# Giving PSUM banks to steps as the order is made, and moving pairs 12 to 15 of an attention stage off TensorE

## The chip, the cores and the metric

The kernel runs on one core of a Trainium2 chip. The metric is the time of one execution on the device in microseconds (us). Executions of one kernel differ by 1 to 2% here, so each comparison below rests on several runs of both kernels on the same chip. (A run is called slow when it took over 1.5% longer than the fastest of the same kernel in its rounds.) Matmul results are written to PSUM; SBUF holds the kernel's other tiles. TensorE is called PE, VectorE DVE, ScalarE ACT, GpSimd POOL, as in the profile.

## The reference

```python
# q, k, v: (8, 8, 576, 64) float32: 8 batches, 8 heads, 576 tokens, 64 wide
# 1. q, k, v are averaged over groups of 4 tokens: an attention over 144 tokens,
#    its output repeated 4 times
# 2. a local attention: token i sees tokens i-3 .. i+3 (masked softmax)
# 3. x = (1 + 2), laid out as 4608 tokens x 512
# 4. h = x @ w_in (512 x 2048);  g = h - tanh(h);  y = g @ w_out (2048 x 512)
```

Two heads of a batch are handled together, as a "pair": 32 pairs, four to a batch. Steps 1 to 3 are the *attention*, step 4 is the *dense* part: nine blocks of 512 tokens, 1152 matmuls of 512 columns.

## The kernel before

The author writes every step as an operation with an estimated time, the buffers that it reads and writes, and a priority. A small list scheduler in the kernel's own Python makes one fixed order from them. A recording layer below (the tile framework) takes the instructions in that order and works out from the tiles that they touch which engine must wait for which semaphore.

The kernel uses PSUM as eight banks of 512 float32 columns each. Before, they have roles, and each role is a tile of its own:

```python
    ps_ts = fixed("ps_ts", [128, 2, 512], FP32, pool=psum)      # two banks: transposes, scores
    ps_ox = fixed("ps_ox", [128, 2, 512], FP32, pool=psum)      # two banks: outputs, transposes back
    # at the start two more pairs, ps_ts1 and ps_ox1; later, in their place:
        ps_hy.extend(fixed("ps_hy", [128, 512], FP32, 4, pool=pool))   # four banks for dense groups
```

One pair of heads goes through these steps (cut):

```python
    qr  <- cast and reorder of q, k              # POOL
    if p >= T_DMA:  qT <- DMA transpose of qr;  qk <- ACT copy
    else:           nine PE transposes into ps_ts;  qk <- ACT copy
    half, qkd <- q and k pooled over four tokens # POOL (DVE too for the first four pairs)
    scores -> ps_ts (from pair NEW on: all scores at once, over ps_ts and ps_ox)
    E <- exp                                     # ACT, reads two banks in one instruction
    E <- E * mask                                # DVE, pair 4 on: both inputs in SBUF
    outs -> ps_ox                                # PE
    r <- 1 / sums; ln <- outs * r                # DVE, each reads two banks in one instruction
    if p >= X_DMA:  lT <- DMA transpose of ln;  xT <- join of lT   # DVE or POOL
    else:           PE transposes into ps_ox; od <- ACT; xT <- DVE
    # the pooled v: PE matmuls with `pick` before pair NEW, adds on POOL from there on
    M2_FIRST, T_DMA, X_DMA, NEW, LATE = 12, 16, 16, 16, 0
```

The pooled q and k are written as two planes:

```python
    qkd = fixed("qkd", [128, 344], BF16, 2)
    eng.tensor_tensor(out=qkd[s][:, 0:2 * G].rearrange("p (i g) -> p g i", i=2),
                      in0=half[:, :, 0, :], in1=half[:, :, 1, :], op=ALU.add)
```

A dense group is four matmuls into one bank of `ps_hy`, a tanh on ACT that reads it, and a subtraction on DVE that reads it again; the second product gathers 16 matmuls in a bank and ACT copies it out.

The softmax here doesn't subtract the row's maximum and nothing guards it: scores larger than these inputs give would overflow.

## Time and profile before

| | before |
|---|---|
| time, median of 3 runs | 347.96 us (346.37 to 349.49) |
| span of the profiled run | 345.8 us |
| first dense matmul | 30.0 us |
| PE idle after it, in gaps of 0.2 us or more | 8.2 us in 6 gaps |

The page of the profile starts with busy times. Part 2 cuts the span into 40 slices; the PE row is the busy share in tenths, the PEclk row the granted TensorE clock in tenths. The last line is part 4, the chain of waits followed back from the end.

```profile
span 345.8 us, 6564 instructions
PE 323.4 (94%) x2479; PEld 164.9 (48%) x2520; DVE 218.5 (63%) x336; ACT 202.7 (59%) x334; POOL 182.9 (53%) x196
...
PE   8777999999969999899989998999999999999995
...
PEclk9998999999998999999999999999999999999999
...
PE 80%; DVE 7%; DMA 4%; ACT 4%; issue 2%; POOL 1%; DVEq 0%; ACTq 0%; POOLq 0%
```

PE is the limit and nearly full. What it loses, it loses at the start and in a few gaps.

The groups of instructions (line, engine, operation, tiles, shape, count; then busy us and mean ns of one, then idle time before them and its releasers) show two things: the mask multiply (L554, L568) and the pooled add (L495).

```profile
L495 POOL TENSOR_TENSOR qkd<-half 128x288 bf16<-128x288 f32 x30 | 46.0, 1535 | 3.2 <-DVE half L490 2.3
L554 DVE TENSOR_TENSOR E<-E,mask 128x960 bf16<-128x960 bf16 x28 | 34.1, 1216 | 14.6 <-ACT E L550 14.4
L568 DVE TENSOR_TENSOR E<-E,mask 128x192 bf16<-128x192 bf16 x28 | 17.3, 619 | 6.0 <-ACT E L561 5.7
L495 DVE TENSOR_TENSOR qkd<-half 128x288 bf16<-128x288 f32 x2 | 4.0, 2022 | 0.1
```

The timeline around one of the gaps (start us, duration us, engine, line, operation; in brackets the idle time before it and what ended it):

```profile
140.41 0.72 POOL L381 CAST vw<-vst 128x640 bf16<-128x640 f32 x1
...
140.47 3.58 DVE L554 TENSOR_TENSOR E<-E,mask 128x960 bf16<-128x960 bf16 x1 [0.17 <-ACT E L550]
...
141.09 1.49 POOL L495 TENSOR_TENSOR qkd<-half 128x288 bf16<-128x288 f32 x1
...
142.16 1.37 POOL L448 CAST qr<-qkn 128x1152 bf16<-128x1152 f32 x1
...
144.10 0.37 PE L579 MATMUL ps_ox<-vw,E 128*128 128x65 bf16 x5 [1.54 <-DVE E L554]
```

The multiply took 3.58 us; the shortest of its line took 0.65 us. It ended half a microsecond after an unbroken run of GpSimd instructions ended, and PE stood still for it.

### The profile page before, as it was taken

To read this page: it belongs to the slowest core of one execution; us is meant where nothing else is said; L and a number is where in the kernel's file an instruction comes from. 1 tells how busy PE (TensorE), PEld (TensorE's weight loads), DVE (VectorE), ACT (ScalarE), POOL (GpSimd) and SP (SyncE) were. 2 spreads that over 40 slices of the span, in tenths; PEclk is the share of its full clock that TensorE was granted. 3 is DMA by queue.
4 is the path that set the end of the run, shared out by engine and by line. 5 is a ranking of instruction groups with operands and counts; after the bars stand their busy time and mean duration, and the time that the engine had idled before them with its cause. 6 is when DMAs were issued, how large, how long until landed. Compare 5 with 4: busy or idle time off the path is not lost.

```text
span 345.8 us, 6564 instructions
## 1 busy us (share of the span) xinstructions
PE 323.4 (94%) x2479; PEld 164.9 (48%) x2520; DVE 218.5 (63%) x336; ACT 202.7 (59%) x334; POOL 182.9 (53%) x196
## 2 busy tenths in 40 slices
PE   8777999999969999899989998999999999999995
PEld 3453455555535555344444444454444444444442
DVE  4775885468876775859887987776765443344300
ACT  2864875668855866576666676677654444344411
POOL 7675748577677792859786978885600100000000
PEclk9998999999998999999999999999999999999999
DMA  7999999898537892999999999662321200110021
GB/s 238 287 262 207 240 255 242 224 303 223 155 104 198 219 240 79 233 203 243 237 247 230 237 239 228 138 139 61 81 59 48 72 32 30 51 40 32 30 83 68
DMA packets 99212, 56.51 MB, mean 163 GB/s; under 512 B 77678, under 2 KB 86382, under 8 KB 99182
## 3 DMA queue, kind: packets, MB, share of 16 engines
q1 hardware_dynamic: 94670, 51.32, 60.3%
q0 software_dynamic: 4224, 4.19, 7.4%
q10 hardware_dynamic: 288, 0.59, 0.6%
q8 instruction: 19, 0.31, 0.4%
q14 instruction: 11, 0.09, 0.1%
HBM read 42.46 MB, written 9.44 MB: 150 GB/s over the span
## 4 chain that ended last, share of the span: by engine, by line
PE 80%; DVE 7%; DMA 4%; ACT 4%; issue 2%; POOL 1%; DVEq 0%; ACTq 0%; POOLq 0%
PE ps_hy L661 34%; PE ps_hy L688 31%; DVE E L554 3%; PE ps_ox L579 3%; DMA w_out_sb<-in_moe_w_out_dram 3%; PE ps_ts L509 3%; PE ps_ts L476 2%; PE ps_ox L586 2%; PE ps_ts L837 2%; DMA out_dram<-y 2%; DVE qkd L495 1%; ACT qk L480 1%; PE ps_ox L614 1%; DVE E L568 1%; PE ps_ox L420 1%
## 5 line engine op out<-in xcount | busy, mean ns | idle before, releaser
L661 PE MATMUL ps_hy<-xT,w_in_sb 128*128 128x512 bf16 x562 | 144.5, 384 | 2.7 <-DVE xT L641 1.5
L688 PE MATMUL ps_hy<-w_out_sb,gT 128*128 128x512 bf16 x550 | 138.4, 379 | 1.9 <-DMA w_out_sb<-in_moe_w_out_dram 0.5
L672 DVE TENSOR_TENSOR gT<-ps_hy,u 128x512 bf16<-128x512 f32 x144 | 97.0, 686 | 66.5 <-ACT u L669 65.5
L669 ACT ACTIVATE u<-ps_hy 128x512 f32<-128x512 f32 x144 | 85.0, 599 | 89.8 <-PE ps_hy L661 89.5
L688 PEld LDWEIGHTS <-gT 128*128 128x128 bf16 x576 | 54.0, 98 | 62.8 <-issue 0.8
L661 PEld LDWEIGHTS <-w_in_sb 128*128 128x128 bf16 x576 | 54.1, 98 | 62.6 <-issue 3.8
L495 POOL TENSOR_TENSOR qkd<-half 128x288 bf16<-128x288 f32 x30 | 46.0, 1535 | 3.2 <-DVE half L490 2.3
L490 POOL TENSOR_TENSOR half<-qk 128x576 f32<-128x576 bf16 x29 | 34.7, 1198 | 18.9 <-ACT qk L480 13.9
L554 DVE TENSOR_TENSOR E<-E,mask 128x960 bf16<-128x960 bf16 x28 | 34.1, 1216 | 14.6 <-ACT E L550 14.4
L448 POOL CAST qr<-qkn 128x1152 bf16<-128x1152 f32 x28 | 33.7, 1204 | 14.7 <-PE ps_ts L476 9.2
L600 DVE TENSOR_TENSOR ln<-ps_ox,r 128x896 bf16<-128x896 f32 x30 | 32.6, 1088 | 0.8
L699 ACT COPY y<-ps_hy 128x512 f32<-128x512 f32 x36 | 21.1, 586 | 18.4 <-PE ps_hy L688 18.4
L550 ACT ACTIVATE E<-ps_ts 128x960 bf16<-128x960 f32 x30 | 29.1, 970 | 4.6 <-PE ps_ts L509 4.6
L381 POOL CAST vw<-vst 128x640 bf16<-128x640 f32 x32 | 26.4, 826 | 2.6 <-PE ps_ox L579 2.0
L480 ACT COPY qk<-ps_ts 128x1152 bf16<-128x1152 bf16 x14 | 15.7, 1118 | 14.6 <-PE ps_ts L476 14.6
L406 POOL TENSOR_TENSOR vp<-v 72x256 bf16<-72x256 f32 x16 | 12.4, 773 | 21.1 <-PE ps_ox L586 21.1
L579 PE MATMUL ps_ox<-vw,E 128*128 128x65 bf16 x300 | 18.9, 196 | 4.2 <-DVE E L554 4.2
L579 PEld LDWEIGHTS <-E 128*128 128x128 bf16 x320 | 16.4, 99 | 11.2 <-DVE E L554 5.7
L568 DVE TENSOR_TENSOR E<-E,mask 128x192 bf16<-128x192 bf16 x28 | 17.3, 619 | 6.0 <-ACT E L561 5.7
L402 POOL TENSOR_TENSOR v<-v 72x512 f32<-72x512 f32 x16 | 20.3, 1268 | 1.0
L467 ACT COPY qk<-qT 128x1152 bf16<-128x1152 bf16 x16 | 19.3, 1207 | 0.0
L624 POOL TENSOR_TENSOR xT<-lT 128x480 bf16<-128x480 bf16 x7 | 7.1, 1009 | 23.1 <-DMA lT<-ln 23.1
(89 smaller groups left out, 254.4 us busy)
## 6 DMA issues: line engine op xcount, KB each, us to landing
vst<-in_v_dram SPq DMA_DIRECT2D x62, 160.0 KB, 4.4
qkn<-in_q_dram SPq DMA_DIRECT2D x32, 288.0 KB, 4.7
out_dram<-y SPq DMA_DIRECT2D x36, 256.0 KB, 2.0
qkn<-in_k_dram SPq DMA_DIRECT2D x30, 288.0 KB, 4.8
v<-in_v_dram SPq DMA_DIRECT2D x16, 288.0 KB
w_in_sb<-in_moe_w_in_dram POOLq DMA_DIRECT2D x4, 512.0 KB, 10.5
w_out_sb<-in_moe_w_out_dram POOLq DMA_DIRECT2D x4, 512.0 KB, 9.6
qkn<-in_k_dram ACTq DMA_DIRECT2D x2, 288.0 KB
```

Source lines behind the costliest of these rows:

```text
L381: P.choice([(eng, ns, lambda fn=fn: fn(out=vw[w][:, 2 * jj:2 * jj + 2, :, 0:64], in_=vst[s])) for eng, ns, fn in CAST_V[p >= NEARLY]], rea ...
L448: op("POOL", 1300, lambda: GP.tensor_copy(out=qr[s].rearrange("p a (h d) -> p h a d", h=2), in_=qkn[sn].rearrange("p h (a d) -> p h a d", ...
L490: eng.tensor_tensor(out=half, in0=four[:, :, 0:2, :], in1=four[:, :, 2:4, :], op=ALU.add)
L495: eng.tensor_tensor(out=qkd[s][:, 0:2 * G].rearrange("p (i g) -> p g i", i=2), in0=half[:, :, 0, :], in1=half[:, :, 1, :], op=ALU.add)
L550: op("ACT", 960, lambda: A.activation(out=e1, in_=ps[:, :, 0:480], func=AF.Exp, scale=SCALE), reads=ts, writes=[("E", e, 0)], pri=pri)
L554: op("DVE", 950, lambda: V.tensor_tensor(out=e1, in0=e1, in1=mask[:, 0:480].unsqueeze(1).to_broadcast([128, 2, 480]), op=ALU.mult), reads= ...
L579: T.matmul(po[:, hh, 65 * t:65 * t + 65], E[e][:, c:c + 128], vw[w][:, 2 * jj + hh, t, :], start=True, stop=True)
L600: op("DVE", 1060, lambda: V.tensor_tensor(out=ln[s].rearrange("p n (h d) -> p h n d", d=D), in0=blocks[:, :, :, 0:64], in1=r[s].unsqueeze( ...
L661: T.matmul(ps_hy[slot], w_in_sb[:, dc, fc * 128:(fc + 1) * 128], xT[dc][:, kb * 512:kb * 512 + 512], start=(dc == 0), stop=(dc == N_DC - 1))
L669: op("ACT", 590, lambda: A.activation(out=u[us], in_=ps_hy[slot], func=AF.Tanh), reads=[("hy", slot)], writes=[("u", us)], pri=DPRI)
L672: op("DVE", 670, lambda: V.tensor_tensor(out=gT[g][:, fc, :], in0=ps_hy[slot], in1=u[us], op=ALU.subtract), reads=[("hy", slot), ("u", us) ...
L688: T.matmul(ps_hy[slot], gT[g][:, fc, ts * 128:ts * 128 + 128], w_out_sb[:, fc, :], start=(fc == 0), stop=(fc == N_FF - 1))
```

## The change

The intent: no fixed roles for banks. While the order is made, each step that fills PSUM is given the bank or the two banks that became free first, up to four banks for attention after the start ("b") and five for dense groups ("d"). With that the first pairs can overlap more, and priorities are set towards the end of batch 0, so that dense work starts sooner. Pairs 12 to 15 are also moved to the form that pairs 16 and later have. The diff, cut to its core:

```diff
+class Banks:
+    def __init__(self, n, kind, key): ...
@@ order(): when a step fills a bank for the first time
+                if t.first == i:
+                    t.at = sorted(sorted((gone_at[x], x) for x in range(8)
+                                         if gone_at[x] <= now)[n][1] for n in range(t.n))
+                    for x in t.at:
+                        gone_at[x], owner[x] = 1e9, t.kind
@@ the tiles
-    ps_ts = fixed("ps_ts", [128, 2, 512], FP32, pool=psum)
-    ps_ox = fixed("ps_ox", [128, 2, 512], FP32, pool=psum)
-    ps_hy = []                    # ... and ps_ts1, ps_ox1, dense_banks()
+    bank = fixed("bank", [128, 8, 512], FP32, pool=psum)
+
+    def one(tok):
+        return bank[:, tok.at[0]]
+
+    def two(tok):
+        a, b = tok.at
+        return bank[:, a:b + 1:b - a]
@@ pooled q and k, interleaved instead of two planes
-    qkd = fixed("qkd", [128, 344], BF16, 2)
+    qkd = fixed("qkd", [128, G + 56, 2], BF16, 2)
-                eng.tensor_tensor(out=qkd[s][:, 0:2 * G].rearrange("p (i g) -> p g i", i=2),
+                eng.tensor_tensor(out=qkd[s][:, 0:G],
@@ q/k transposes in two parts (5 and 4 of nine), one bank each, copied by ACT or (start) DVE
@@ back(): matmuls with the identity and with `up` (each row repeated 4 times) add the two
   attentions in PSUM; the copies of od and the add on DVE become one copy on DVE or ACT
@@
-    M2_FIRST, T_DMA, X_DMA, NEW, LATE = 12, 16, 16, 16, 0
+    M2_FIRST, T_DMA, X_DMA, NEW, LATE = 16, 12, 12, 12, 0
+    P.cap = {"b": 4, "d": 5}
+    P.goal = {("x", 0, j) for j in range(NP)}
```

(Cut: the search for free banks, the priorities along the path to batch 0, the order of the first loads, the filler matmuls in PE's idle stretches.)

## The prediction

> **What bounds the kernel now.** TensorE. The page gives PE 94% busy, and the chain of waits gives PE 80% of the span, 65% on the two dense matmul lines. From the PE timeline the span of 345.8 us splits into:
> - start, until the first dense matmul: 30.0 us;
> - dense work: 1152 matmuls of 512 columns at 216 ns (47 took 10.14 us near the end) = 248.8 us;
> - PE idle after 30 us: about 10 us. Four gaps hold most of it: 3.5 us at 101-104, 1.54 at 144, 1.33 at 178, 1.33 at 212;
> - two stretches of granted clock near 0.5 (30-33.4, and 104-107.5, after the largest gap): about 3.4 us lost;
> - tail after the last matmul: 3.8 us;
> - the rest, about 50 us: attention steps on PE.
>
> DMA (share near 1.1 over 140-220 us) and GpSimd (78% there) are busy but not the limit: attention is done by about 270 us, and PE then works off a backlog of dense blocks without a gap. So shorter PE work, a sooner start and fewer gaps should all reach the end.
>
> **What makes the gaps.** Each ends with a DVE mask multiply of E that took 3.2 to 3.6 us, where the median for its line is 0.68 (960 columns) or 0.46 us (192). GpSimd ran without a pause during each. [...] PE, in its fixed order, waits.
>
> **What the change does.**
> 1. Pairs 12-15 lose nine PE transposes (0.50 us a pair), the transposes back (0.53) and half of a V pooling by matmul (0.34): 4 x 1.37 = -5.5 us of PE.
> 2. Pairs 0-11 get transposes back as matmuls which add the upsampled part: 1216 columns against 720, about +0.1 us of PE each, +1 in all. The small ACT copy of od goes.
> 3. The pooled q and k are written interleaved, not as two planes. That add took 1.54 us on GpSimd (30 times) and 2.0 on DVE for 288 elements, while a 576-element add takes 1.20 and 0.93. I estimate 0.8 and 0.45: -22 us of GpSimd. Two of the DVE ones and one GpSimd one lie in the chain of the start, 5.4 us together: about -3 there.
> 4. Pooling V for pairs 12-15 on GpSimd costs 4 x 2.04 = +8 us.
> 5. Banks by step instead of by role, split q/k transposes and priorities towards batch 0 shorten the start further, about -1 us. Five banks for dense groups give little: PE runs gapless with four after 265 us.
> 6. DMA gets eight more transposes, in a stage (80-140 us) whose share is only 0.6-0.7.
>
> **Sum.** Start 26; dense 248.8; attention on PE 45; gaps 5 (GpSimd lighter, order new, lock still there); clock 1.7; tail 3.8: span 330.3. The run took 1.7 us more than its span: 332 us. Range 324 to 342. Faster by over 2%: 0.86; within 2%: 0.11; slower: 0.03.
>
> **What would show it.** First dense matmul near 26 us; the pooled add near 0.8 us on GpSimd; GpSimd busy near 170 us; PE gaps after the start near 5 us in sum; no half clock at the dense start; PE gapless in the last 80 us.
>
> **What would make it wrong.** The order is made from estimated times: if one is off, PE waits in order and gaps come back, with more GpSimd work at pairs 12-15 (the lock). The interleaved add may not be faster. With banks shared, attention may lose banks to dense groups and batch 1 come late, so PE runs out of dense work at 40-65 us.

"The lock" is from here on a name for what the trace of the kernel before shows: a DVE instruction with both inputs in SBUF can take much longer while GpSimd runs. Of the 28 large mask multiplies (L554), the ten in whose time GpSimd ran no instruction took 0.65 to 0.66 us; the five longest took 2.33 to 3.58 us, and GpSimd ran for 1.8 to 3.4 us of each. What in the hardware holds them up is not shown.

## More of the kernel before

From the table of waits (engine, tile and line that waited, who released it: us in total, times, longest) the reader should keep how the attention's PSUM readers wait before: the reciprocal for the outputs, the exp for the scores, each for the step that fills its own banks.

```profile
DVE r L598 <- PE ps_ox L586: 8.2, 9, 1.6
...
ACT E L550 <- PE ps_ts L509: 4.6, 16, 1.2
```

## The result, and the profile after

The changed kernel took 387.65 us, median of 3 runs (383.62 to 387.89), against 347.96: the ratio is 1.1105, 95% interval 1.0968 to 1.1242. (Ratios here are the mean time of one kernel's fast runs over the mean of the other's fast runs of the same rounds, so not quite the ratio of the medians that are quoted.) It is 11% slower where 4.6% faster was predicted.

The same lines of the page, changed kernel:

```profile
span 386.2 us, 6562 instructions
PE 332.4 (86%) x2461; PEld 160.1 (41%) x2461; DVE 205.5 (53%) x327; ACT 201.6 (52%) x331; POOL 178.2 (46%) x217
...
PE   7779979798899688769788889887759999999995
...
PEclk9996998999999999999999999999999999999999
```

PE has about as many matmuls as before and is at 86%; in the second quarter and the third most slices are at 6 to 8 tenths. No other engine is fuller than before: this is waiting, not work. (The chain of waits stops after a quarter of this span, so the table of waits is used.)

The groups that answer to those of before:

```profile
L614 DVE TENSOR_TENSOR E<-E,mask 128x960 bf16<-128x960 bf16 x28 | 33.2, 1185 | 32.8 <-ACT E L610 32.8
...
L557 POOL TENSOR_TENSOR qkd<-half 128x288 bf16<-128x288 f32 x29 | 20.5, 708 | 1.8 <-DVE r L658 1.3
L557 DVE TENSOR_TENSOR qkd<-half 128x288 bf16<-128x288 f32 x3 | 2.1, 684 | 0.1
```

The pooled add did become more than twice as fast on GpSimd (1535 to 708 ns). The mask multiply is no slower than before. So the loss is elsewhere, and the waits show it:

```profile
ACT E L610 <- PE bank L748: 10.7, 6, 3.9
ACT u L730 <- DVE ln L660: 10.1, 6, 2.8
PE bank L748 <- DVE ln L660: 9.7, 8, 1.5
ACT E L610 <- PE bank L594: 9.2, 6, 3.3
...
DVE r L658 <- PE bank L722: 8.8, 6, 1.9
DVE r L658 <- PE bank L645: 8.6, 7, 1.9
ACT E L610 <- PE bank L722: 7.8, 5, 4.2
PE bank L748 <- ACT E L610: 7.4, 8, 1.1
```

L722 and L748 are the dense matmuls. L610 is the exp of the scores, L658 and L660 are the reciprocal and the scaling of the attention's output. An exp has no business waiting for a dense matmul: it reads scores that L572 wrote. A dense tanh (L730) waits for the attention's ln, although both only read PSUM, for different data. Such pairs do not occur in the waits of the kernel before.

One case in the timeline:

```profile
129.43 0.32 PE L638 MATMUL bank<-vw,E 128*128 128x65 bf16 x5
...
129.71 0.59 PE L722 MATMUL bank<-xT,w_in_sb 128*128 128x512 bf16 x2
...
130.41 0.25 DVE L658 RECIPROCAL r<-bank 128x14 f32<-128x14 f32 x1 [1.89 <-PE bank L722]
...
130.71 0.59 PE L722 MATMUL bank<-xT,w_in_sb 128*128 128x512 bf16 x2 [0.41 <-DVE r L658]
...
131.78 1.09 DVE L660 TENSOR_TENSOR ln<-bank,r 128x896 bf16<-128x896 f32 x1 [0.57 <-PE bank L748]
...
132.92 0.38 PE L748 MATMUL bank<-w_out_sb,gT 128*128 128x512 bf16 x1 [1.18 <-DVE ln L660]
```

The outputs (L638 and its neighbour L645) were done at about 129.9. The reciprocal started at 130.41, as soon as two dense matmuls were done. The next two dense matmuls waited for the reciprocal; ln waited for the next ones; and PE then stood 1.18 us until ln was done. Dense work and attention take turns.

The compiled program says which banks these are. This is the 14th reciprocal and its ln, the ones above:

```
r  L658 reads banks 1 and 7; waits until PE has finished L722 in bank 5
ln L660 reads banks 1 and 7; waits until PE has finished L748 in bank 6
```

Banks 5 and 6 lie between 1 and 7. The view `bank[:, 1:8:6]` touches banks 1 and 7 alone, but the recording layer treats it as if it touched all from 1 to 7, and orders everything that lies between. Why the layer makes a dense tanh wait for another instruction that only reads is not shown here. But the two had no bank in common; the waits were drawn too wide.

I counted such waits in the compiled programs, among all waits for PE, ACT, DVE or GpSimd: a wait is counted when nothing in the last group of instructions that it waits for shares a bank or a buffer with the waiting instruction. Before: 5 of 1344. Changed kernel: 190 of 1399.

### Where the time went

The span of each profile below is split from the PE timeline. "Gaps" are idle stretches of 0.2 us or more after the first dense matmul; "clock" is half of the time after it at a granted clock of 0.5 (in the changed kernel dense matmuls started 427 ns apart at 0.5, from 32.2 us on, and 216 ns apart at 1.0, from 35.5 us on); "rest" is what remains: PE at work, with stalls too short to show. (A dense matmul is drawn some 380 ns long though the next one starts 216 ns after it, so a stall of up to 0.16 us hides in "busy".)

| kernel | span | start | gaps | clock | rest | tail |
|---|---|---|---|---|---|---|
| before | 345.8 | 30.0 | 8.2 | 3.3 | 300.5 | 3.7 |
| changed | 386.2 | 29.6 | 40.4 | 6.3 | 305.5 | 4.5 |
| b_one | 342.1 | 27.8 | 7.8 | 3.4 | 299.4 | 3.7 |
| b_apart | 405.7 | 27.5 | 62.2 | 1.7 | 310.5 | 3.7 |
| adj | 337.7 | 25.4 | 8.6 | 3.4 | 296.0 | 4.4 |
| adj_16 | 337.8 | 25.4 | 4.3 | 0.0 | 303.9 | 4.1 |
| b_12 | 355.9 | 29.5 | 20.1 | 6.8 | 295.1 | 4.5 |
| adj_7 | 340.7 | 26.0 | 9.3 | 5.1 | 295.8 | 4.4 |
| adj_ps | 334.7 | 26.3 | 6.0 | 1.7 | 296.3 | 4.4 |
| adj_ps16 | 339.8 | 26.1 | 6.4 | 0.0 | 303.6 | 3.7 |

The lower rows are the experiments.

### The profile page after: what moved, and what is told of

The parts are those of the page before. It is cut to its first block, busy times and chain, and to the rows that moved or that the text cites. A ratio compares the mean times of both kernels' runs of the same rounds, so it can differ in the third digit from the quotient of the medians.

```text
span 386.2 us, 6562 instructions
## 1 busy us (share of the span) xinstructions
PE 332.4 (86%) x2461; PEld 160.1 (41%) x2461; DVE 205.5 (53%) x327; ACT 201.6 (52%) x331; POOL 178.2 (46%) x217
## 5 line engine op out<-in xcount | busy, mean ns | idle before, releaser
L748 PE MATMUL bank<-w_out_sb,gT 128*128 128x512 bf16 x576 | 146.2, 381 | 24.3 <-DVE ln L660 9.7
L722 PE MATMUL bank<-xT,w_in_sb 128*128 128x512 bf16 x576 | 148.9, 388 | 11.5 <-ACT E L610 3.2
L733 DVE TENSOR_TENSOR gT<-bank,u 128x512 bf16<-128x512 f32 x144 | 96.5, 685 | 74.6 <-ACT u L730 60.1
L730 ACT ACTIVATE u<-bank 128x512 f32<-128x512 f32 x144 | 84.7, 598 | 89.3 <-PE bank L722 71.5
L748 PEld LDWEIGHTS <-gT 128*128 128x128 bf16 x576 | 54.2, 98 | 90.7 <-issue 31.3
L722 PEld LDWEIGHTS <-w_in_sb 128*128 128x128 bf16 x576 | 54.6, 99 | 80.3 <-issue 21.7
L610 ACT ACTIVATE E<-bank 128x960 bf16<-128x960 f32 x32 | 31.1, 973 | 34.4 <-PE bank L748 10.7
L660 DVE TENSOR_TENSOR ln<-bank,r 128x896 bf16<-128x896 f32 x32 | 34.8, 1089 | 6.6 <-PE bank L748 2.0
L759 ACT COPY y<-bank 128x512 f32<-128x512 f32 x36 | 21.1, 586 | 21.1 <-PE bank L748 20.2
L638 PE MATMUL bank<-vw,E 128*128 128x65 bf16 x320 | 19.7, 194 | 3.9 <-DVE E L614 0.9
L625 ACT ACTIVATE E<-bank 128x576 bf16<-128x576 f32 x32 | 20.9, 652 | 4.3 <-PE bank L645 1.6
L658 DVE RECIPROCAL r<-bank 128x14 f32<-128x14 f32 x32 | 7.8, 244 | 25.7 <-PE bank L722 8.8
L557 POOL TENSOR_TENSOR qkd<-half 128x288 bf16<-128x288 f32 x29 | 20.5, 708 | 1.8 <-DVE r L658 1.3
L638 PEld LDWEIGHTS <-E 128*128 128x128 bf16 x320 | 16.3, 98 | 11.5 <-issue 2.8
```

The lines of the kernel that those rows point to most:

```text
L610: op("ACT", 960, lambda: A.activation(out=e1, in_=two(t1)[:, :, 0:480], func=AF.Exp, scale=SCALE), drain=[t1], writes=[("E", e, 0)], pri=pri)
L638: T.matmul(two(to)[:, hh, 65 * t:65 * t + 65], E[e][:, c:c + 128], vw[w][:, 2 * jj + hh, t, :], start=True, stop=True)
L660: op("DVE", 1060, lambda: V.tensor_tensor(out=ln[s].rearrange("p n (h d) -> p h n d", d=D), in0=blocks()[:, :, :, 0:64], in1=r[s].unsqueez ...
L722: T.matmul(one(tok), w_in_sb[:, dc, fc * 128:(fc + 1) * 128], xT[dc][:, kb * 512:kb * 512 + 512], start=(dc == 0), stop=(dc == N_DC - 1))
L730: op("ACT", 590, lambda: A.activation(out=u[us], in_=one(tok), func=AF.Tanh), drain=[tok], writes=[("u", us)], pri=DPRI)
L733: op("DVE", 670, lambda: V.tensor_tensor(out=gT[g][:, fc, :], in0=one(tok), in1=u[us], op=ALU.subtract), drain=[tok], reads=[("u", us)], w ...
```

## The experiments

**Theory A**: the loss is waits between steps with no bank in common, because a two-bank view counts as all the banks between. **Theory B**: it is the handing of banks between attention and dense groups, with an order made from wrong estimates; which two banks does not matter. **Theory C**: it is the move of pairs 12 to 15.

### adj: the changed kernel with neighbouring banks

```diff
@@ order(): two-bank steps
-                    t.at = sorted(sorted((gone_at[x], x) for x in range(8)
-                                         if gone_at[x] <= now)[n][1] for n in range(t.n))
+    # an aligned pair (0,1), (2,3), (4,5) or (6,7); single banks by preference where the
+    # neighbour is in use; room() asks the same question
+                t.at = where        # from fit(now, ...)
```

> The changed kernel, but each two-bank step gets two neighbouring banks (an aligned pair) instead of any two free ones. Theory A (waits between steps that share no bank: a view of banks a and b counts as touching all banks between them, as all banks are one tile): the waits with nothing in common fall from 190 to 6 of about 1400, PE idle between 32 and 300 us falls from about 43 us to under 15, time 328 to 345 us. Theory B (handing banks from attention steps to dense groups couples PE to attention, and the order's estimated times are off; which two banks does not matter): stays above 375 us with dense matmuls waiting for DVE and ACT. Theory C (pairs 12-15 on DMA and GpSimd are what costs): above 375 us too.

Measured: correct, 339.19 us median (337.49 to 340.95, 4 runs), ratio to before 0.9801 (0.9693 to 0.9909). Waits with nothing in common fell from 190 to 6. The 48.5 us of span between the changed kernel and adj are, by the table, 31.8 of gaps, 9.5 of rest, 4.2 of start, 2.9 of clock. Attention's readers again wait for their own banks, and no dense matmul waits for the attention's ln:

```profile
ACT E L632 <- PE bank L594: 14.8, 15, 1.9
...
DVE r L680 <- PE bank L667: 7.6, 9, 2.3
```

(L594 are the scores, L667 the outputs.) This speaks for A and against B and C: banks are still handed over, five are still open to dense groups, pairs 12 to 15 are still moved. But with other banks the scheduler also makes another order, so this alone is not the cleanest test.

### b_one and b_apart: the kernel before, with other bank numbers and nothing else

```diff
@@ b_one: one tile, the same pairs as neighbours
+    bank = fixed("bank", [128, 8, 512], FP32, pool=psum)
+    def duo(a, b):
+        return bank[:, a:b + 1:b - a]
+    ps_ts = duo(0, 1)
+    ps_ox = duo(2, 3)               # dense groups: banks 4, 5, 6, 7
@@ b_apart: after the first four pairs
-    ps_ox = duo(2, 3)               # dense groups: 4, 5, 6, 7
+    ps_ox = duo(2, 7)               # dense groups: 3, 4, 5, 6
```

Every engine's instructions stand in the same order in the two; only bank numbers differ.

> Control: the kernel before, its six bank tiles made one tile of eight banks, each pair of banks still neighbouring; every engine's order is the same. Theory A: waits with nothing in common 3, time within 1% of before (346 to 350 us). B and C: the same.

> As the control, but after the start the second attention pair of banks is banks 2 and 7, and the dense groups have 3 to 6, which lie between. Every engine's instructions and order are those of the control. Theory A: 194 waits with nothing in common, time 365 to 400 us, dense matmuls waiting for DVE ln and ACT exp as in the changed kernel. B and C: within 1% of the control, since no bank is handed over and pairs 12-15 are as before.

Measured: b_one 345.64 us median (343.49 to 348.16), ratio 0.9989 (0.9852 to 1.0127). b_apart 406.53 us median of 4 runs; its three fast runs took 405.53 to 407.43; ratio 1.1736 (1.1592 to 1.1881). The waits of b_apart (L666 and L693 are the dense matmuls, L605 the ln, L603 the reciprocal, L674 the tanh):

```profile
ACT u L674 <- DVE ln L605: 35.8, 13, 3.3
...
PE bank L693 <- DVE ln L605: 17.8, 14, 2.1
PE bank L666 <- DVE ln L605: 16.9, 14, 1.5
...
DVE r L603 <- PE bank L693: 16.2, 12, 1.6
```

That settles A's mechanism. In b_apart no bank is handed over, the order is that of the kernel before, and pairs 12 to 15 are as they were; two banks that lie apart cost 60 us, a little more than what I had given as the upper end (400). The instructions that read the two banks are hardly slower for it themselves: ln took 1089 ns on average in b_one and 1092 in b_apart, the reciprocal 244 and 250. One tile in place of six costs nothing that these runs could tell from noise.

### b_12: the move of pairs 12 to 15 alone

```diff
-    M2_FIRST, T_DMA, X_DMA, NEW, LATE = 12, 16, 16, 16, 0
+    M2_FIRST, T_DMA, X_DMA, NEW, LATE = 12, 12, 12, 12, 0
```

> The kernel before with only the number changed from 16 to 12: pairs 12-15 take DMA transposes, merged scores and V pooled on GpSimd. A (and the prediction's step 1): PE work 5.5 us less, time 340 to 346 us. C: slower than before by over 5 us.

Measured: 357.62 us median (354.97 to 359.76), ratio 1.0327 (1.0164 to 1.0491). My expectation was wrong, C's was right for this part. The PE work did fall as predicted (rest 300.5 to 295.1, that is 5.4 us), but gaps rose from 8.2 to 20.1 us and the clock loss from 3.3 to 6.8. GpSimd was busy 198.3 us in place of 182.9, and DVE's mask multiplies got longer: 1380 ns on average for the large one in place of 1216. So the move has a cost of its own, which is not the 11% of the change but eats what the move saves. The theory for it is the **lock** of which the prediction speaks: that what lengthens a DVE instruction with two SBUF inputs (the large multiply took 0.65 us at the shortest and 3.58 at the longest in the kernel before) is GpSimd running at the same time.

### adj_16, b_q, b_12q, adj_qr: less GpSimd work

```diff
@@ adj_16: adj, and
-    M2_FIRST, T_DMA, X_DMA, NEW, LATE = 16, 12, 12, 12, 0
+    M2_FIRST, T_DMA, X_DMA, NEW, LATE = 16, 16, 16, 16, 0
@@ b_q: before, with only the interleaved qkd (od moved into an idle tile for space)
+    qkd = fixed("qkd", [128, G + 56, 2], BF16, 2)
@@ b_12q: b_q with 12 in place of 16
@@ adj_qr: adj, the reordering cast
-            op("POOL", 1300, ...)
+            P.choice([("POOL", 1300, GP.tensor_copy), ("ACT", 1250, A.copy)], ...)
```

> The neighbouring-bank version with pairs 12-15 back on PE transposes and pooling by matmul (12 changed to 16). Prediction's step 1 (PE work is what counts): 4 x 1.37 = 5.5 us slower than adj, about 345 us. Lock theory (GpSimd work at pairs 12-15 gives back what PE saves): within 1% of adj, 336 to 342 us, with fewer PE gaps between 100 and 180 us than adj's 8 us.

> The kernel before with the pooled q and k written interleaved and nothing else of the change (od moved into an unused tile for space); each engine keeps its order of operations. Prediction's step 3: the pooled add falls from 1.5 to 0.7 us on GpSimd and from 2.0 to 0.45 on DVE, first dense matmul about 3 us sooner, GpSimd busy about 22 us less. Lock theory: PE gaps after 30 us also fall, from 10 us to under 6; together 338 to 343 us. If GpSimd time does not matter: only the start, 344 to 346 us.

> b_q with pairs 12-15 moved (16 changed to 12). b_12 without the interleaving was 3% slower than before, with PE gaps of 24 us instead of 10. Lock theory: with 22 us less of GpSimd work the move costs little: within 1.5% of b_q, PE gaps under 15 us. Rival (the order with 12 is bad of itself, or DMA is what hurts): still 10 us slower than b_q.

> adj with the cast that reorders q and k (1.18 us, 28 times on GpSimd) offered to ACT as well, so the order puts a part of them there. Lock theory: GpSimd busy falls by 10 to 20 us, DVE instructions blocked for over 2 us get rarer, PE gaps after 30 us fall from 9.7 to under 6: 331 to 337 us. Rival (gaps come from the order's wrong estimates whatever GpSimd does, or ACT becomes the limit): 338 us or more.

(These expectations count PE's idle time otherwise than the table of gaps does: 24 and 10 us where it has 20.1 and 8.2.)

| | median us | ratio to before (95%) |
|---|---|---|
| adj_16 | 340.69 | 0.9792 (0.9726 to 0.9859) |
| b_q | 341.96 | 0.9738 (0.9653 to 0.9822) |
| b_12q | 345.78 | 0.9867 (0.9793 to 0.9941) |
| adj_qr | 344.26 | 0.9884 (0.9815 to 0.9954) |

adj_16 is as fast as adj, as the lock theory expected. By the table above, adj has 7.9 us less of rest than adj_16 and gives back 4.3 in gaps, 3.4 in clock and 0.3 in tail: nothing is left.

b_q shows that the interleaved pooled add, with no other part of the change, is worth 2.6% by its two fast runs. (The medians of all runs, slow ones included, give 1.7%. Two of its four runs were slow, and so was its profile; the add took 728 ns on GpSimd.)

b_12q is within 1.5% of b_q, against 3.3% that the same move cost without the interleaving. That fits the lock theory, but each of the two has only two fast runs and their intervals overlap, so this alone does not show it; the profile is again a slow one.

adj_qr is a miss. GpSimd was busy 164.5 us in place of 177.0, yet gaps were 12.5 us in place of 8.6 and the kernel is 0.8% slower by the ratios to before. Its gaps end with other releasers too (the pooled add once, a join on GpSimd once, ACT several times): with the cast on ACT the order is a new one, with new waits. DVE instructions of over 2 us did get rarer, as expected (4 in place of 6), but what that saved was lost to the new order: this run does not separate the two. So the lock had to be tested in a way that leaves the order alone.

### adj_7 and adj_ps: the lock taken away, with the order the same

A lock of this kind is visible in adj too. GpSimd works from 149.40 to 154.14 without a pause, and a DVE instruction with two SBUF inputs, whose median in the kernel before was 0.65 us, takes 4.15:

```profile
149.40 1.26 POOL L482 TENSOR_TENSOR v<-v 72x512 f32<-72x512 f32 x1
...
150.51 4.15 DVE L713 TENSOR_TENSOR xT<-lT 128x480 bf16<-128x480 bf16 x1 [0.83 <-DMA lT<-ln]
150.61 1.14 POOL L525 CAST qr<-qkn 128x1152 bf16<-128x1152 f32 x1
...
151.72 1.14 POOL L574 TENSOR_TENSOR half<-qk 128x576 f32<-128x576 bf16 x1
...
153.48 0.66 POOL L579 TENSOR_TENSOR qkd<-half 128x288 bf16<-128x288 f32 x1
...
155.48 0.23 PE L594 MATMUL bank<-qk 64*128 64x96 bf16 x1 [4.56 <-DVE gT L755]
```

The DVE instructions of the kernel before that read one input from PSUM and one from SBUF kept their length: ln took 1070 to 1093 ns in all 32 cases, with GpSimd at work during 27 of them, and gT 621 to 694 ns in all 144. This suggests a test: the mask is put in PSUM. adj_7 is the control: bank 7 is reserved, a bf16 copy of the mask is made there by PE transposes, and the joins go to GpSimd alone. adj_ps differs from it in two operands:

```diff
-                in1=mask[:, 0:480].unsqueeze(1).to_broadcast([128, 2, 480]),
+                in1=pmask[:, 0:480].unsqueeze(1).to_broadcast([128, 2, 480]),
-                in1=mask[:, 480:576].unsqueeze(1).to_broadcast([128, 2, 96]),
+                in1=pmask[:, 480:576].unsqueeze(1).to_broadcast([128, 2, 96]),
```

> Control for the next run: adj with bank 7 kept out of use, a copy of the mask put there at the start but not read, and the last joins on GpSimd only. Lock theory: the mask multiply on DVE still reads two SBUF tensors, so blocked ones of 2 to 4 us stay (over 15 us of excess over the shortest); seven banks cost little: 336 to 348 us.

> The same with every engine's order the same, but the mask multiplies read the mask from bank 7 in PSUM, so they have one SBUF input. Lock theory: no mask multiply takes over 1.5 us[...]; PE gaps after the first dense matmul fall below half of adj_7's; 5 to 12 us faster than adj_7. Rival (the gaps come from wrong estimates in the order, and the long multiplies are only a symptom): within 1% of adj_7.

Measured: adj_7 339.24 us median (337.62 to 342.41), ratio to before 0.9786. adj_ps 335.13 us (332.67 to 336.94), ratio 0.9652 (0.9558 to 0.9746). By the means of the four runs of each, adj_ps is 4.7 us faster (339.63 to 334.97), and no run of the one lies among those of the other. The groups of adj_7, then of adj_ps:

```profile
L636 DVE TENSOR_TENSOR E<-E,mask 128x960 bf16<-128x960 bf16 x28 | 30.9, 1104 | 33.3 <-ACT E L632 33.3
L651 DVE TENSOR_TENSOR E<-E,mask 128x192 bf16<-128x192 bf16 x28 | 21.9, 784 | 1.7 <-ACT E L644 1.3
```

```profile
L636 DVE TENSOR_TENSOR E<-E,bank 128x960 bf16<-128x960 bf16 x28 | 18.3, 653 | 32.5 <-ACT E L632 32.5
L651 DVE TENSOR_TENSOR E<-E,bank 128x192 bf16<-128x192 bf16 x28 | 6.9, 248 | 5.3 <-ACT E L644 5.1
```

With the mask in PSUM the multiplies take 653 and 248 ns on average, where the shortest with two SBUF inputs took 648 and 240 in the kernel before. The lock is shown as far as these runs go: same order, same GpSimd work, one operand in PSUM in place of SBUF, and the large multiply takes 653 ns on average in place of 1104, the small one 248 in place of 784. GpSimd gains too: its same instructions are busy for 182.8 us in place of 189.3. Gaps fell from 9.3 to 6.0 us and the clock loss from 5.1 to 1.7. The gaps did not fall below half, as I had expected: one of 3.33 us is left, in which PE waits for the pooled add on GpSimd, and that is not the lock. (adj_7's largest gap, 3.83 us behind a blocked multiply, is gone; this one comes a pair later, behind five GpSimd instructions that each take their usual time, 0.66 to 1.26 us.) The gain is slightly below the range of 5 to 12 us.

### adj_ps16: does the move pay once the lock is gone?

> adj_ps with pairs 12-15 back on PE (12 changed to 16). If the lock is what took back the 5.5 us of PE work that moving these pairs saves (adj and adj_16 were equal), adj_ps is now 4 to 7 us faster than adj_ps16. If it was something else (DMA, the order), the two stay within 1%.

Measured: 340.95 us median (339.19 to 341.93), ratio to before 0.9808. adj_ps is 5.8 us faster by the means of the runs (340.8 to 335.0). With the lock, the move of pairs 12 to 15 was worth nothing (adj against adj_16); without it, it is worth what PE no longer does: the table has 7.3 us less of rest, of which 1.7 of clock and 0.7 of tail are given back, while gaps are the same within 0.4.

### adj_d4: the fifth bank for dense groups

```diff
-    P.cap = {"b": 4, "d": 5}
+    P.cap = {"b": 4, "d": 4}
```

> adj with at most four banks for dense groups instead of five. Prediction's step 5 (five banks give little): within 1% of adj, 336 to 342 us. If the fifth bank matters: over 343 us.

Measured: 343.31 us median of 4 runs; the first run slow (374.91 us at a clock of 0.849). The three fast runs took 341.51 to 344.82, ratio to before 0.9875 (0.977 to 0.998). That is 0.8% more than adj by the ratios; the mean of the fast runs (342.7) lies between my two expectations, their median (341.81) inside the first, and the intervals overlap: what the fifth bank is worth stays open, but it is not much.

## Why the prediction was wrong

**The step that failed is point 5**, "Banks by step instead of by role ... shorten the start further, about -1 us". It treated a bank as the thing that is waited for, and so took the freedom to give any two banks to a step as free. What is waited for is what the recording layer believes a view touches. With one tile and a view over two banks apart, that is every bank between. The runs show its size in place of -1 us: +48.5 us of span (changed kernel against adj, whose order differs too), and 60 us where the same is done, with the order kept, to the kernel before (b_apart against b_one). In the prediction's sum the term that broke is "gaps 5": 40.4 us were measured, 35 of the 56 us by which the span exceeds the predicted 330.3. Another 11.7 are in what PE does (305.5 for the predicted 248.8 and 45), where stalls too short to show are counted, 4.6 in the clock. Among "what would make it wrong" I named banks that attention loses to dense groups; that was not it either, as adj hands over banks just the same. The diff showed the line, and the roles before were tiles of their own: the question to ask was what the waits are made from.

**The start (26 us) was right in size and lost in the change.** With neighbouring banks the first dense matmul comes at 25.4 us. In the changed kernel it came at 29.6: there too the compiled program has such waits (the fourth ln reads banks 2 and 4 and waits for a step in bank 3). Of the other signs that the prediction named, PE was without gaps in the last 80 us, but the dense work began at half clock (28.6 to 35.4 us).

**The pooled add was right on GpSimd**, estimated 0.8 us and measured 0.71; on DVE the estimate of 0.45 was too low (0.68). Alone it is worth 2.6% by two fast runs (b_q). GpSimd's busy time, predicted near 170 us, was 178.2 in the changed kernel and 177.0 in adj.

**The PE work of pairs 12 to 15 was right** (5.5 us predicted; 5.4 in b_12, 7 to 8 in the later versions), **but that it would reach the end was wrong.** The prediction said that "shorter PE work, a sooner start and fewer gaps should all reach the end" and let gaps fall to 5 us because GpSimd gets lighter in total. So a second step failed: with the lock there, less PE work need not reach the end. In b_12 the move costs 3.3%, in adj it costs what it saves, and in adj_ps, with the mask multiplies free of the lock, it pays. Which of the moved work does the blocking is not shown: in b_12 the multiply that took 4.41 us at 111.1 stood behind casts and a q/k add alone (L381, L495, L448), the one of 2.90 us at 93.3 behind V pooling too (L402).

**The lock itself was read rightly** from the durations in the trace before, and adj_ps shows it (1104 to 653 ns for the large multiply). How the hardware comes to it is not shown.

**The transposes back as matmuls** were predicted at +0.1 us of PE a pair. Summed from start to start in the PE timeline after the first dense matmul, they take 9.1 us for 12 pairs in adj_16 and 6.8 before: 0.19 us a pair more.

**The sum, corrected.** adj is the change as it was meant, and took 339 us: inside the predicted range (324 to 342), 7 us over the predicted 332. By its span, 3.6 us of that are gaps, 1.7 clock and 2.2 PE work; the largest gap, 4.56 us, is the one shown above behind a blocked DVE instruction, but how much of the rest the lock causes is not shown. adj_ps took 335.1 us and beats both kernels, by 3.5% and by more than 13% (387.65 to 335.13).

**What stays open.** The remaining gap of 3.3 us in adj_ps, the worth of the fifth dense bank, and what in adj_qr's order made it slower than adj. That the changed kernel's own order would be fast without the false waits is shown only indirectly, as neighbouring banks also change the order.

## What to carry to other kernels

When buffers become slices of one large tile, look at what the dependency tracking makes of the slices, before trusting a schedule that treats them as independent: a view with a step may count as everything that it spans. The sign in a profile is a wait between two instructions that share no data, above all between two that only read; make such views contiguous, or give the parts tiles of their own. And before moving work to an idle GpSimd, look at which DVE instructions with two SBUF inputs run at that time: the move may cost more there than it saves elsewhere (in b_12 it made the kernel 3.3% slower), and taking one operand from PSUM brought the 56 multiplies here from 1104 and 784 ns on average to 653 and 248.

## What else the runs show, and leave open

- A view over two banks with a step was treated as all banks between: 190 of 1399 waits in the changed kernel in place of 6 in adj, and 194 in b_apart in place of 3 in b_one, worth 48 to 60 us.
- In these traces a DVE instruction with two SBUF inputs can stay long through several GpSimd instructions in a row: 4.15 us in place of 0.65, behind five, in adj. GpSimd need not pause to end it: in the kernel before, the multiply that took 3.16 us from 100.08 on (0.24 at the shortest) ended at 103.24 by the profile, when GpSimd's next instruction had already begun (103.10).
- In the changed kernel the clock was at half from 28.6, 59.3 and 171.9 us on, for 13.7 us before the last matmul by the clock records, and the longest gap between the first dense matmul and the last of them was 1.53 us. Gaps of that size do not decide it by themselves: b_apart had 70 gaps, 62.2 us in all and up to 2.08 us long, and before its last matmul only one stretch at half clock, of 3.4 us. What does decide it stays open.
